# Two steps for the outputs of a chunk: a one-element read by ScalarE in place of a drain of TensorE

## Chip, cores and metric

The kernel runs on one core of a Trainium2 chip. The metric is the device time of one execution in microseconds. Before the change three runs took 586.36, 588.10 and 589.55 us, median 588.1.

## What is computed

A DeltaNet recurrence over 768 tokens for 4 batches of 8 heads of size 48, and then a multiplicative feed-forward block over the 3072 tokens that it yields:

```python
def _attn_ref(q, k, v, beta):               # (4, 8, 768, 48), beta (4, 8, 768)
    k_n = k / (np.linalg.norm(k, axis=-1, keepdims=True) + 1e-06)
    state = np.zeros((B, H, D, D), dtype=np.float32)
    for t in range(S):
        kt, vt, bt = (k_n[:, :, t], v[:, :, t], beta[:, :, t, None])
        y[:, :, t] = np.einsum('bhd,bhde->bhe', q[:, :, t], state)
        v_old = np.einsum('bhde,bhd->bhe', state, kt)
        state = state + bt[:, :, :, None] * np.einsum('bhd,bhe->bhde', kt, vt - v_old)

def _moe_ref(x, w1, w2, w3, w_out):         # x (3072, 384), w1 and w2 384 x 1024
    return ((x @ w1) * (x @ w2) @ w3) @ w_out
```

## The kernel before

**Tiling.** The 768 tokens are cut into 12 chunks of 64 (`c` or `m` in the code). Two chunks make a unit `u` of 512 tokens (4 batches times 128), with which the feed-forward block works. Within a chunk the recurrence is written in matrix form: scores K K^T and K Q^T, the inverse of a triangular matrix, the product of that inverse with (V minus K times the state), the new state, and the outputs.

**Order.** Every part of the work is a Python generator that yields after each step. The string `ORDER` names the parts in the order in which their steps are issued: a letter for the part and a number for the chunk, unit or block. `step` runs one step, and `in_text_order` (L177) chains the instructions of each engine in this order, so no scheduler moves them. Each engine works through its own queue in this order and waits for the others by semaphores; the DMAs are issued by SP, in its own order.

The parts that matter here:
- `s` scores (L378): for each of two halves r a group of 48-row TensorE products (L388, L394) into a bank pair, then VectorE takes U (L400) and PT (L418) out of it.
- `e` corner (L500) completes the inverse with small TensorE products (L522), `c` chain (L567) makes the state's products, the product of the inverse (R times T) and the new state, all at L575 with two or three bank pairs.
- `y` outputs (L639), the part that is changed.
- `V` inverse of 32x32 blocks, on VectorE (L462, L469).
- `b`, `a` products of x with w1 and w2 (L808), with copies by ScalarE (L823) and multiplications by VectorE (L827).
- `A`, `B` (L888 to L942) the same for a pair of 128-row blocks of w1 or w2 with eleven half products in place of more (a Strassen-like scheme): TensorE L897, ScalarE L902 to L918, VectorE L922 and L928. They need the sums of `m` (L876 by GpSimd, L879 by VectorE).
- `S` sums of slabs by GpSimd (L1000), `o` products with the folded weights w3 w_out (L1028), `x` results (VectorE L1059, ScalarE L1063 and L1065) and their stores (L1045, SP).
- `f` fold of w3 and w_out (L788, copies by ScalarE L795), `t` transposes (L779), `k`, `q`, `v`, `p`, `P` loads.

**Banks.** `two_banks` (L164) hands out one of two PSUM bank pairs in turn, `bank` (L167) one of four single banks in turn. A part that takes a pair waits, by the framework's dependences, until all readers of the pair's last contents are done. The scores, the corner, the chain and the outputs all take pairs; the first two inverses hold one of the two for a time.

**Tiled and dense products.** The recurrence's products have at most 64 rows and columns of weights; TensorE works four of them at a time in its quadrants (here "tiled"). The feed-forward block's products use 128 x 128 weights ("dense").

**The outputs.** y of chunk c is the sum of two things: Q times the state (48 rows, L672, operands `KQ,S`) and PT times X (64 rows, operands `PT,X`). The sums of a bank may come from products that lie in different row halves of TensorE. The kernel therefore makes two lists, `modes`: the first has the state products of the lower half and all PT products, the second the state products of the upper half. All products of the first list are issued, then a drain of TensorE (L670), and then the second list. In the next step of the part ScalarE copies the sums into xT in eight pieces (L693), and in a third (chunk 0 and every odd chunk) SP issues six DMAs that move rows within xT (L704), which GpSimd's and VectorE's sums (L876, L879) and the first products of the next pairs (L897) read. Chunk 0 has no state, so only its first list holds products; its drain has nothing behind it.

A product is two instructions for TensorE (a weight load and a matmul, each issued twice for float32), so the first list is 32 + 64 instructions and the second 32.

Of the kernel before, what the change touches and what calls it, by code (L numbers as in the profile page):

```python
# [8 lines left out]
FP32 = mybir.dt.float32  # L9
# [27 lines left out]


ORDER = """
k0 g0 beta beta g0 g0 P0 K0 C1 beta C1 g0 C0 C0 q0 k1 g0 K0 P4 K1 g0 g0 g0 K0 K0 C9 C9 C0 K1 C8  # L40
C1 P5 C8 K1 k2 C8 K1 g0 K1 K0 q1 C10 C11 t0 t0 Q0 Q0 P1 C10 Q0 Q0 Q0 k3 C11 g0 Q1 Q1 Q1 C9 t1
N0 C10 P6 Q1 Q1 N0 g1 C11 P9 C3 C2 C3 g1 C3 g1 s0 C2 C2 P2 s0 s0 s0 t3 C13 C12 C12 C18 N0 s0 g1
C19 C12 s0 s0 s1 s1 t1 C18 C5 t2 t2 q3 s1 C19 u0 C13 C13 C18 g1 P3 t3 C6 s1 s1 C19 s1 u1 P8 f0
C7 t4 C5 V0 V0 t5 g1 C4 C7 C4 v0 C5 g1 C4 C6 C6 C7 f1 P7 V0 f0 n0 C17 C17 v1 V0 V0 V0 V0 V0 V0
V0 V0 V0 V0 V0 V0 V0 V0 V0 V0 V0 C16 P10 C16 t4 V0 t5 V0 V0 V0 V0 f0 f1 f1 C17 t10 t10 V0 V0 V0
t11 K2 s1 C14 t11 K2 f5 f5 C15 V0 C15 C16 V0 C14 V0 g1 V0 K2 t9 V0 K2 f5 P11 C20 V0 C14 C20 V0
t8 C15 t9 K2 f2 q2 f2 V0 C21 n0 C23 C21 V0 C21 Q3 V0 f2 t8 Q3 Q3 V0 V0 V0 V0 V0 V0 V0 V0 V0 V0
V0 V0 V0 V0 V0 V0 V0 V0 V0 V0 V0 V0 t13 t6 V0 V0 V0 V0 t13 f4 P13 f4 t6 C26 C20 Q3 Q3 g1 t12
P12 f4 t7 V0 V0 V0 V0 g1 V0 Q2 t12 N1 t7 Q2 C27 K3 Q2 Q2 e0 C27 Q2 e0 C22 C22 C26 f6 s2 e0 s2
e0 C23 K3 e1 s2 f3 C24 K3 C23 K3 e0 s0 C25 s2 C25 e0 C22 p4 C26 V1 s2 c0 s2 u2 C24 e1 e1 C27 c0  # L50
P14 t15 e1 c0 y0 K3 c0 y0 s3 s3 s3 t14 s3 f3 C29 s3 u3 e1 s3 t14 V1 c1 C24 e1 f6 V1 n1 n1 c1 c1
c1 f6 V1 V1 V1 V1 V1 C28 f7 t15 f7 f7 C28 C28 C29 s1 y1 V1 V1 V1 V1 f3 y0 b0 C25 C29 b0 y1 b5
V1 b6 b6 P15 V1 V1 V1 V1 V1 V1 V1 V1 V1 V1 V1 V1 V1 V1 V1 V1 V1 V1 b5 P16 y1 b7 v2 b3 b1 C30 b7
b2 P17 C32 n2 b3 n2 V1 V1 V1 V1 V1 V1 V1 V1 V1 V1 V1 V1 c1 d4 V1 a05 V1 V1 b1 a02 V1 V1 V1 V1
V1 C31 a02 V1 k4 b2 V1 V1 V1 V1 V1 V1 V1 a05 a06 V1 b4 a04 a04 b4 V1 a07 C30 C30 C32 C32 a06
a00 V1 V1 V1 V1 V1 V1 a01 V1 V1 a07 a03 c1 d4 C34 a00 c2 C34 C35 C35 C34 a01 C31 C33 C33 b3 C33
C31 a03 a03 C35 a01 p4 e2 a03 b1 a01 T T b3 T b1 a00 b0 e2 e2 e2 d4 b0 N1 a00 b6 c2 e2 g2 b5 d4
b5 T v3 n3 n3 W2 e2 e3 N1 c2 b4 b6 c2 a05 y2 e3 b4 a05 a04 a04 y2 k5 a07 g2 g2 g2 g2 e3 W2 c2
a07 b7 b2 e3 e3 c2 c3 a06 g2 g2 g2 S0 p5 b7 g2 d5 d5 p5 k6 c3 V2 e3 S0 b2 c3 c3 a02 g2 a02 y3
o0 W2 N2 s4 W1 a06 W1 W1 y3 s4 y3 s4 s4 s4 o0 u4 d5 d5 s5 s4 s5 S0 S0 s5 s5 S0 m1 x0 s5 m1 o0  # L60
u5 S0 S0 S0 S0 S0 S0 S0 S0 S0 x0 x0 m1 m1 g3 g3 g3 g3 o0 o0 x0 V2 c3 V2 V2 o0 V2 B10 V2 x0 B10
V2 x0 S0 S0 o0 x0 V2 V2 V2 x0 V2 B10 V2 B10 x0 B10 B10 B10 B10 B10 x0 V2 V2 A10 v5 V2 A10 B10
B10 A10 A10 A10 A10 B10 A10 V2 B10 p6 A11 A11 A11 A11 A11 A10 A10 V2 A11 V2 V2 V2 V2 V2 A10 A11
A10 A10 A11 A11 A11 A10 d6 A12 A12 k7 v4 A12 A12 A12 d6 A12 A12 A11 V2 V2 V2 A12 A12 A12 V2 V2
A12 V2 A12 B10 B12 B12 A11 B10 p6 B12 V2 A12 B12 B12 B12 B12 V2 x0 V2 V2 B12 V2 B12 W1 A13 A13
B12 B12 A11 B12 B12 B12 B12 N2 V2 N2 A13 d6 A13 e4 s5 c3 n4 d6 A13 p7 B11 B11 B11 B11 B11 B11
B11 B11 g3 g3 g3 g3 B11 B11 B11 c4 n4 A13 S1 g3 B11 e4 e4 e4 c4 A13 A13 A13 e4 g3 A13 N3 e5 A13
e4 s6 c4 s6 s6 c4 A13 y4 a16 B11 d7 y4 s6 d7 p7 e5 e5 a16 N3 B11 B11 o1 A13 s6 u6 S1 N3 s6 n5
n5 e5 c4 d7 a17 d7 c4 a17 S1 x1 s7 s7 s7 V3 s7 s7 o1 c5 s7 e5 S1 o1 S1 S1 S1 S1 c5 e5 c5 S1 S1
S1 c5 u7 V3 S1 S1 o1 x1 V3 V3 V3 V3 S1 y5 p8 o1 x1 S1 V3 V3 V3 V3 x1 y5 o1 V3 c5 V3 V3 V3 v6 x1  # L70
y5 x1 x1 x1 S1 c5 A22 A22 m2 m2 o1 m2 d8 d8 x1 V3 n6 x1 m2 A22 A22 A22 A22 A22 A22 A22 B20 B20
V3 B20 B20 A22 B20 V3 V3 A22 A22 B20 B20 k8 V3 A20 g4 A22 A20 B20 B20 V3 V3 V3 A20 B20 x1 A20
A20 A20 A20 A20 V3 B20 A20 p8 A20 A21 V3 V3 V3 A20 A20 B20 B22 A20 A21 B20 A21 A21 B20 B20 B22
c6 v7 V3 V3 V3 V3 V3 B22 B22 V3 V3 k9 V3 B22 B22 A21 A21 A21 B22 B22 B22 A21 A21 B22 B22 B22
B22 A21 A21 d8 A21 B21 B22 B21 B21 g4 e6 g4 A23 A21 B22 B21 A23 B21 A23 g4 g4 g4 d8 p9 A23 g4
g4 A23 A23 e7 e6 B21 B21 B21 B21 B21 B21 n6 c6 e6 A23 e6 A23 A23 g4 e6 s8 e6 A23 g4 N4 A23 B21
B21 B21 c6 a26 n7 s8 s8 e7 c6 A23 B21 y6 y6 d9 d9 s8 A23 v8 a27 a27 a26 n8 S2 S2 o2 s8 V4 s8 c6
e7 n7 S2 p9 d9 e7 u8 o2 c6 d9 s9 s9 s9 n8 s9 s9 s9 x2 o2 x2 e7 e7 c7 S2 u9 V4 c7 S2 S2 S2 S2 x2
o2 c7 S2 S2 S2 S2 S2 S2 c7 o2 V4 V4 V4 V4 V4 y7 y7 x2 V4 y7 S2 S2 V4 o2 V4 V4 x2 x2 o2 A30 A30
V4 V4 V4 x2 m3 x2 x2 m3 V4 p10 m3 V4 c7 x2 V4 m3 k10 A30 A30 A30 A30 A30 A30 A30 V4 A31 A31 V4  # L80
A31 A30 A30 A30 c7 A31 k11 A31 A31 A32 A31 A31 A31 V4 V4 V4 A31 A31 c8 A31 V4 A30 A32 V4 A32
B30 A31 A32 V4 V4 V4 V4 V4 V4 V4 V4 V4 A32 A32 A32 A32 B30 B30 B30 B30 B30 B30 B30 B30 B30 B30
v9 A32 A32 V4 B30 B32 B30 A32 A32 B30 B32 B32 B30 B32 A32 A33 d10 B32 B32 g5 B32 A33 x2 n9 B32
B32 n9 d10 A33 c8 A33 A33 A33 e8 B32 B32 e8 B32 N4 e8 B32 B32 N4 a36 e8 e8 g5 g5 e8 g5 A33 c8
A33 g5 A33 p10 A33 c8 B31 d10 c8 y8 A33 B31 d10 c8 B31 B32 B31 B31 A33 e9 e9 B31 B31 B31 g5 a36
g5 g5 y8 e9 B31 S3 p11 e9 g5 B31 B31 B31 d11 d11 e9 B31 B31 S3 V5 c9 B31 e9 c9 A33 a37 c9 o3 c9
y9 a37 g5 s10 N5 s10 p11 s10 v10 y9 y9 d11 d11 o3 x3 s10 s11 S3 S3 s10 s10 s11 s11 s11 s11 m4
m4 m4 m4 u10 S3 S3 S3 S3 S3 S3 S3 S3 u11 o3 V5 x3 S3 S3 S3 S3 s11 n10 o3 x3 o3 x3 A40 V5 V5 o3
V5 A40 c9 x3 x3 V5 V5 o3 x3 x3 A40 V5 x3 V5 V5 A40 A40 A40 A40 A40 A40 x3 V5 V5 V5 A40 A43 A43
A43 A40 V5 A40 A43 A43 A43 A40 A43 A43 A43 B40 A43 V5 V5 V5 A43 B40 V5 V5 A43 B40 B40 B40 B40  # L90
A42 A43 V5 V5 V5 V5 A42 B40 B40 B40 B40 A42 A42 A42 A42 B40 B40 A42 a46 A42 V5 V5 B40 B40 B40
B42 A42 A42 c9 v11 a46 A42 V5 B42 A42 A42 V5 V5 B42 B42 V5 V5 B42 V5 V5 V5 V5 e10 A41 B42 n10
B42 B42 B42 A41 A41 B42 B42 B42 B42 B42 x3 A41 A41 A41 c10 A41 B41 A41 B41 A41 A41 A41 B41 c10
A41 n11 e10 B42 B41 B41 B41 B41 B41 B41 B41 e10 B41 S4 B41 B41 B41 e10 e10 e10 S4 a47 A41 e11
e11 B41 e11 a47 e11 c10 N5 N5 o4 c10 x4 e11 c10 c10 e11 o4 o4 S4 S4 S4 S4 n11 S4 S4 S4 y10 y10
x4 c11 o4 c11 c11 S4 S4 S4 S4 S4 o4 c11 x4 y11 S4 S4 x4 y11 o4 x4 x4 o4 y11 A50 A50 x4 x4 m5
# [10 lines left out]
def kernel(  # L107
# [14 lines left out]
    P = 128  # L122
# [5 lines left out]
    NP = H // 2  # L128
# [19 lines left out]
    def feat(z):  # L148
        return slice(C * z, C * z + D)
# [6 lines left out]
    def in_turn(pool, shape, tag, n, name, dt=FP32):  # L156

        i = turns.get(tag, -1)
        while True:
            i = turns[tag] = (i + 1) % n  # L160
            if (tag, i) not in held:
                return pool.tile(shape, dt, tag=f"{tag}{i}", name=name, bufs=1)
# [24 lines left out]

    ident = const.tile([P, P], FP32, name="ident")
    make_identity(nc, ident[:])
    strict = in_turn(ffn, [P, P], "o", 2, "strict")  # L190
    pool.memset(strict[:], 1.0)
    pool.affine_select(
# [72 lines left out]
    sums = {}  # L265
# [373 lines left out]
    def outputs(c):  # L639
# [24 lines left out]
                            x = half((z + h) % 2)  # L664
                            todo.append((h, z, r, X[x, r, h, :], PT[x, r, h, :]))
        part = [(h // NP, (h + z) % 2) for todo in modes for h, z, *_ in todo]
        issued, n = ([], []), 0
        for mode, todo in enumerate(modes):
            if mode:
                drain = pe.drain().ins  # L670
            for h, z, r, lhs, rhs in todo:
                i = pe.matmul(  # L672
                    region(h, z, r), lhsT=lhs, rhs=rhs,
                    start=part[n] not in part[:n], stop=part[n] not in part[n + 1 :],
                )
                issued[mode].append(i.ins)
                n += 1
        for i in issued[0]:
            in_order(i, drain)
        for i in issued[1]:  # L680
            in_order(drain, i)
        yield
        u, cc = divmod(c, 2)
        if cc == 0:
# [529 lines left out]
```

## Time and profile before

| what | value |
|---|---|
| runs, us | 586.36, 588.10, 589.55 |
| profiled execution, us | 585.52 |
| its span, us | 583.8 |
| mean granted TensorE clock | 0.977 |
| L672 `KQ,S`: matmuls | 704 in chunks 1 to 11, 14.8 us busy |
| L672 `PT,X`: matmuls | 768, 14.0 us busy |
| L693 copies to xT by ScalarE | 96, 366 ns each, 30.5 us busy |
| L704 DMAs within xT | 42; to landing 1.9, 2.6, 5.4 us (shortest, median, longest) |
| L1028 products, dense, 192 columns | 330 ns each, issued at a distance of 0.16 us |

The profiled execution took 585.52 us, of which 583.8 are the span from the first to the last instruction. Matmul lengths are modelled and overlap, so that distances between the starts of weight loads (`PEld`) tell more of TensorE's pace than the lengths of its matmuls. In the lists of groups and in timelines, `<-` names what ended the idle time before an instruction.

### The profile page before, as it was taken

What the parts mean: (1) busy time and instruction counts of PE and PEld (TensorE: products, weight loads), DVE (VectorE), ACT (ScalarE), POOL (GpSimd) and SP (SyncE); (2) the same over time, 40 slices, a digit from 0 to 9 for tenths busy, and PEclk for the clock granted to TensorE, in tenths of its full rate; (3) what the DMA queues carried; (4) which work ended last, traced back from release to release, by engine and by line L of the source; (5) the groups of instructions that cost most, each with busy time, mean ns of one, the idle gap of its engine ahead of it and who ended that gap; (6) DMA issues with size and microseconds to landing.
All of it is one profiled execution on the core that took longest, in us unless ns stands there. A gap on an engine that the chain in (4) does not pass through costs nothing.

```text
span 583.8 us, 20142 instructions
## 1 busy us (share of the span) xinstructions
PE 536.8 (92%) x8660; PEld 419.4 (72%) x8660; DVE 357.9 (61%) x828; ACT 194.3 (33%) x449; POOL 222.7 (38%) x284
## 2 busy tenths in 40 slices
PE   4559796899999999999999999999999999989997
PEld 3546464678888975678877688676688767977787
DVE  2645956379546689854898664985485974123522
ACT  2776674344432012331133222123421323323310
POOL 6476407032778703536105371024325043610041
PEclk9669999899999999999999999999999999999999
DMA  8999955778764436444472533455434103010001
GB/s 231 223 274 245 245 121 82 120 143 140 129 94 67 96 74 103 92 58 90 94 124 66 84 47 71 86 122 77 55 66 98 26 37 70 10 50 15 0 1 54
DMA packets 204408, 56.59 MB, mean 97 GB/s; under 512 B 193344, under 2 KB 199488, under 8 KB 202528
## 3 DMA queue, kind: packets, MB, share of 16 engines
q1 hardware_dynamic: 200128, 54.52, 48.0%
q10 hardware_dynamic: 4192, 0.79, 0.9%
q8 instruction: 68, 1.11, 0.8%
q14 instruction: 20, 0.16, 0.1%
HBM read 43.09 MB, written 11.01 MB: 93 GB/s over the span
## 4 chain that ended last, share of the span: by engine, by line
PE 76%; DMA 13%; DVE 3%; ACT 3%; SPq 3%; issue 2%; ACTq 0%; DVEq 0%
PE ps_f L897 29%; PE ps_f L1028 15%; PE ps_f L808 11%; PE ps_w L575 6%; PE ps_w L672 4%; PE ps_f L788 4%; DMA raw<-in_moe_w_dram 3%; PE ps_w L522 3%; DMA X<-in_q_dram 2%; DMA Ub<-Ud 2%; DMA Ud<-U 1%; PE ps_w L388 1%; PE ps_w L394 1%; DMA raw<-in_moe_w_out_dram 1%; DMA vtok<-in_v_dram 1%
## 5 line engine op out<-in xcount | busy, mean ns | idle before, releaser
L1000 POOL TENSOR_TENSOR ab<-ab 128x256 f32<-128x256 f32 x96 | 68.2, 740 | 59.6 <-DVE ab L942 35.1
L942 POOL TENSOR_TENSOR ab<-ab,y 128x512 f32<-128x512 f32 x24 | 30.5, 1272 | 130.3 <-DVE y L922 81.3
L897 PE MATMUL ps_f<-xT,w1s 128*128 128x256 f32 (+1 forms) x200 | 70.3, 471 | 0.3 <-DVE ab L928 0.2
L1028 PE MATMUL ps_f<-w,ab 128*128 128x192 f32 x376 | 66.0, 330 | 4.2 <-DVE osb L1059 4.2
L1028 PEld LDWEIGHTS ps_f<-w,ab 128*128 128x128 f32 x376 | 60.9, 190 | 6.5 <-issue 5.7
L897 PE MATMUL ps_f<-xT,w2s 128*128 128x256 f32 (+1 forms) x160 | 56.3, 468 | 0.1
L897 PEld LDWEIGHTS ps_f<-xT,w1s 128*128 128x128 f32 x200 | 36.8, 190 | 24.7 <-issue 19.4
L693 ACT COPY xT<-ps_w 48x256 f32<-48x256 f32 x96 | 30.5, 366 | 70.5 <-PE ps_w L672 70.0
L1028 PE MATMUL ps_f<-room,ab 128*128 128x192 f32 x272 | 48.2, 331 | 2.4 <-DVE room L1059 2.4
L788 PE MATMUL ps_f<-w2s,w3T 128*128 128x384 f32 x128 | 46.4, 514 | 3.7 <-ACT KQ L368 2.5
L469 DVE TENSOR_TENSOR Vb<-Vb,tb 128x31 f32<-128x31 f32 (+15 forms) x124 | 45.1, 364 | 4.3
L462 DVE TENSOR_TENSOR tb<-Vb,Ub 128x31 f32<-128x31 f32 (+15 forms) x124 | 43.4, 350 | 5.7 <-DMA Ub<-Ud 2.9
L1028 PEld LDWEIGHTS ps_f<-room,ab 128*128 128x128 f32 x272 | 44.0, 190 | 3.8 <-issue 2.4
L808 PE MATMUL ps_f<-xT,w2s 128*128 128x256 f32 (+1 forms) x144 | 45.5, 461 | 0.0
L897 PEld LDWEIGHTS ps_f<-xT,w2s 128*128 128x128 f32 x160 | 29.8, 190 | 19.2 <-issue 15.3
L788 PEld LDWEIGHTS ps_f<-w2s,w3T 128*128 128x128 f32 x128 | 24.5, 198 | 20.4 <-ACT KQ L368 3.1
L808 PEld LDWEIGHTS ps_f<-xT,w2s 128*128 128x128 f32 x144 | 26.1, 189 | 10.6 <-issue 7.7
L388 PE MATMUL ps_w<-KQ 48*64 48x128 f32 x384 | 26.8, 284 | 7.5 <-ACT PT L412 6.3
L740 POOL TENSOR_TENSOR w<-w,raw 128x512 uint32<-128x512 uint32 x16 | 20.4, 1287 | 31.4 <-DVE w L738 27.7
L388 PEld LDWEIGHTS ps_w<-KQ 48*64 48x64 f32 x384 | 22.2, 140 | 11.9 <-ACT PT L412 6.7
L897 PE MATMUL ps_f<-xT,room 128*128 128x256 f32 x100 | 29.8, 385 | 0.1
L561 POOL TENSOR_TENSOR vtok<-vtok,n 128x384 f32<-128x384 f32 x24 | 19.9, 838 | 23.5 <-DMA vtok<-in_v_dram 23.5
(155 smaller groups left out, 983.0 us busy)
## 6 DMA issues: line engine op xcount, KB each, us to landing
raw<-in_moe_w_dram SPq DMA_DIRECT2D x8, 1024.0 KB, 8.2
vtok<-in_v_dram SPq DMA_DIRECT2D x24, 192.0 KB, 4.4
raw<-in_moe_w_dram SPq DMA_DIRECT2D x12, 384.0 KB, 7.7
out_dram<-osb SPq DMA_DIRECT2D x46, 96.0 KB, 1.7
ktok<-in_k_dram SPq DMA_DIRECT2D x44, 96.0 KB, 4.1
raw<-in_moe_w_out_dram SPq DMA_DIRECT2D x4, 768.0 KB, 4.9
Ud<-U SPq DMA_DIRECT2D x48, 64.0 KB, 3.1
Ub<-Ud SPq DMA_DIRECT2D x6, 512.0 KB, 3.8
```

The lines of the kernel that those rows point to most:

```text
L388: pe.matmul(ps[half(z), 0, n : n + 128], lhsT=x[:, 0, :], rhs=x.rearrange("p j t -> p (j t)"), start=True, stop=True,)
L462: dve.tensor_tensor(out=tv, in0=V[:, 0 : s + 1, s : s + 1].to_broadcast([P, s + 1, n]), in1=U[:, s, s + 1 : BS].unsqueeze(1).to_broadcast( ...
L469: dve.tensor_tensor(out=o, in0=o, in1=tv, op=ALU.subtract)
L575: pe.matmul(out(ps, r, h, z), lhsT=lhs(r, h, z), rhs=rhs(r, h, z), start=True, stop=True,)
L672: i = pe.matmul(region(h, z, r), lhsT=lhs, rhs=rhs, start=part[n] not in part[:n], stop=part[n] not in part[n + 1 :],)
L693: act.copy(out=xT[f, p:NP:2, b : b + NR, cc, :].rearrange("p a r t -> p r a t"), in_=pyv[f, z, b : b + NR],)
L788: pe.matmul(ps[:, 0:DM], lhsT=w3Ts[jc, kc // 4][:, kc % 4 * P : kc % 4 * P + P], rhs=wo[:, kc], start=(kc == 0), stop=(kc == KF - 1),)
L808: pe.matmul(ps[:].rearrange("p b c t -> p b (c t)"), lhsT=w[:, m, js], rhs=x[:, m, :, c0:c1].rearrange("p b c t -> p b (c t)"), start=(m = ...
L897: pe.matmul(ps, lhsT=lhs, rhs=rhs, start=start, stop=stop, skip_group_check=not start)
L942: (dve if u == last else pool).tensor_tensor(out=t, in0=t, in1=y[i], op=ALU.mult)
L1000: pool.tensor_tensor(out=o_, in0=x_, in1=y_, op=op)
L1028: pe.matmul(ps[b][:, b, :], lhsT=abs_[u, HF * f + i][:, t0 : t0 + P], rhs=ws_[w][:, i], start=first and i == 0 and (b == 0 or n == "F"), s ...
```

## The change

The drain goes. For chunks with a state (1 to 11) `outputs` has two more steps: after the first list it yields; then ScalarE copies one element of the region that the last product of the first list wrote into a small tile, `seen`, and yields; then the second list is issued, its first product with a dependence on that read. The other steps follow as before. Since the second list now adds onto finished groups, the `stop` flags are set at the end of the first list, and the second list skips the check of groups.

```diff
+    seen = const.tile([P, 1], FP32, name="seen")
...
-        issued, n = ([], []), 0
+        n = 0
         for mode, todo in enumerate(modes):
-            if mode:
-                drain = pe.drain().ins
-            for h, z, r, lhs, rhs in todo:
+            if mode and todo:
+                yield
+                h, z, r = modes[0][-1][:3]
+                read = act.copy(
+                    out=seen[feat(h // NP)][0:1], in_=region(h, z, r)[0:1, 0:1]
+                ).ins
+                yield
+            for x, (h, z, r, lhs, rhs) in enumerate(todo):
                 i = pe.matmul(
                     region(h, z, r), lhsT=lhs, rhs=rhs,
-                    start=part[n] not in part[:n], stop=part[n] not in part[n + 1 :],
-                )
-                issued[mode].append(i.ins)
+                    start=part[n] not in part[:n],
+                    stop=part[n] not in part[n + 1 : len(modes[0]) if mode == 0 else None],
+                    skip_group_check=mode == 1,
+                ).ins
+                if mode and x == 0:
+                    tc.add_manual_dep(
+                        i, read.name,
+                        mybir.DependencyInfo(mybir.DependencyClass.Sync, mybir.DependencyReason.DATA),
+                        reason="sums of both modes",
+                    )
                 n += 1
-        for i in issued[0]:
-            in_order(i, drain)
-        for i in issued[1]:
-            in_order(drain, i)
         yield
```

`ORDER` keeps all other tokens in their order and gets 22 more `y` tokens. The first list and the read stand where the whole step stood; the second list stands some tokens later, and the copies where they stood or, where that would be ahead of the second list, behind it. Two places, before and after (`y3` has its DMAs as a last step, `y9` too):

```
before  y3 o0 W2 N2 s4 W1 a06 W1 W1 y3 s4 y3 s4 s4 s4
after   y3 y3 o0 y3 W2 N2 s4 W1 a06 W1 W1 y3 s4 y3 s4 s4 s4

before  y9 a37 g5 s10 N5 s10 p11 s10 v10 y9 y9 d11 d11 o3 x3 s10 s11
after   y9 y9 a37 g5 s10 N5 s10 p11 s10 v10 d11 d11 o3 y9 y9 y9 x3 s10 s11
```

What lies on TensorE between the first and the second list, and what follows the second list:

| chunk | between | behind |
|---|---|---|
| 1 | 3 dense products (b, 256 columns) | dense (b) |
| 2 | 3 dense (a, 256) | 3 dense (a), corner products, then the state's (L575) |
| 3 | 8 dense (o, 192) | scores, first and second half |
| 4 | 3 dense (a, 512) | scores, second half, then corner products (L522) |
| 5 | 8 dense (o, 192) | dense (o), L575, then the first pair product (L897) |
| 6 | scores (first half), 3 dense (a, 512) | 8 dense (o), then the state's (L575) |
| 7 | 8 dense (o, 192) | dense (o), then the first pair product (L897) |
| 8 | 2 dense (pair, 256) | dense (pair) |
| 9 | scores (first half), 8 dense (o, 192) | scores, second half, and of the next chunk |
| 10 | L575 (state), 8 dense (o, 192) | L575 (R times T) |
| 11 | 8 dense (o, 192) | dense (o), then the first pair product (L897) |

The orders of SP, VectorE and GpSimd are unchanged; ScalarE has the eleven reads more, in chunk 1 between two fold copies (L795), and in chunk 10 a copy of a result (L1065) stands ahead of the eight copies in place of behind them, in chunk 8 the order of the eight copies and the pair's copies is as before.

## Prediction, made before the run

> **What bounds the kernel now.** I read the page first: its busy shares, the 40 slices and the chain of work that ended last.
>
> ```profile
> span 583.8 us, 20142 instructions
> PE 536.8 (92%) x8660; PEld 419.4 (72%) x8660; DVE 357.9 (61%) x828; ACT 194.3 (33%) x449; POOL 222.7 (38%) x284
> PE   4559796899999999999999999999999999989997
> ...
> PE 76%; DMA 13%; DVE 3%; ACT 3%; SPq 3%; issue 2%; ACTq 0%; DVEq 0%
> ```
>
> TensorE is busy nine tenths or more in almost every slice (14.6 us each) from the ninth on, and three quarters of the chain are its own work. So a microsecond in which TensorE stands still after about 100 us is a microsecond of the result, unless it falls where TensorE waits anyway. All eleven drains (chunks 1 to 11) lie behind 124 us.
>
> Next, one drain from near: the timeline of weight loads (PEld) around chunk 9, and ScalarE's in the same stretch. Columns are start, length, engine, line, operation, operands, shapes, count.
>
> ```profile
> 425.23 0.52 PEld L672 LDWEIGHTS ps_w<-KQ,S 48*48 48x48 f32 x32 [0.23 <-PE ps_f L1028]
> 425.66 0.98 PEld L672 LDWEIGHTS ps_w<-PT,X 64*48 64x48 f32 x64
> 426.90 0.52 PEld L672 LDWEIGHTS ps_w<-KQ,S 48*48 48x48 f32 x32 [0.26 <-issue]
> ...
> 428.43 2.57 PEld L1028 LDWEIGHTS ps_f<-room,ab 128*128 128x128 f32 x16
> 431.23 0.14 PEld L388 LDWEIGHTS ps_w<-KQ 48*64 48x64 f32 x2 [0.23 <-issue]
> ```
>
> ```profile
> 427.64 2.59 ACT L693 COPY xT<-ps_w 48x256 f32<-48x256 f32 x8 [8.70 <-PE ps_w L672]
> ```
>
> The first sums are the first two rows, the second sums the third. A load takes 0.12, so the last load of the first sums starts at 425.66 + 0.98 - 0.12 = 426.52 and the next one at 426.90: the drain makes this distance 0.38, where the first two rows join at 0.03. The dense L1028 loads (0.19 each) end with one that starts at 430.81; the tiled L388 follows 0.42 later, though dense loads of this form follow each other at 0.16. A change between dense and tiled products is thus paid too. Eight copies of 2.59 in all empty the bank pair: from the first load of the second sums (426.90) to the end of the copies (430.23) it is 3.33.
>
> **The change on TensorE alone.** Eleven distances of 0.38 go: -4.18. In chunks 1, 2, 5, 6, 7, 8 and 11 the second sums become a tiled group of their own between dense products. Such a group costs, beside its own loads, 0.52 (last dense load of 256 columns to the first tiled one) + 0.20 (tiled to dense) + 0.11 (first to second dense load), less the two dense distances of 0.22 that would stand there: 0.40, and the same with 192 and 512 columns (0.42 and 0.95 in place of 0.52, with 0.16 and 0.43). Seven of them: +2.8. In chunks 3, 4, 9 and 10 the second sums join tiled work that follows (four joints of 0.03: +0.1). Sum -1.3. The places below are worked out with absolute starts, so this sum is inside them and isn't added again. ScalarE's eleven reads of one element have no row; the nearest are its copies, 0.37 for 256 columns and 0.48 for 384, so 0 to 0.37 each; I take 0.2. ScalarE is mostly idle at those places (8.70 in the row above), and at least two dense products on TensorE cover each read.
>
> **What moves: the copies.** They start 0.74 after the first load of the second sums (426.90 to 427.64), now later by a whole dense group, and two things wait for them.
>
> First, the bank pair. There are two, taken in turn, so the second taker after a chunk's outputs needs its pair. Chunk 0 shows the rule at work, with TensorE idle:
>
> ```profile
> 105.16 2.59 ACT L693 COPY xT<-ps_w 48x256 f32<-48x256 f32 x8 [4.26 <-PE ps_w L672]
> ```
> ```profile
> 106.70 0.66 PE L779 MATMUL ps_f<-ident,w 128*128 128x128 f32 x4
> 107.81 0.33 PE L388 MATMUL ps_w<-KQ 48*64 48x128 f32 x2 [0.45 <-ACT xT L693]
> ```
>
> The copies end at 107.75, all eight of them, and the scores start at 107.81. So the second taker starts no earlier than 3.33 + 0.06 = 3.39 after the first load of the second sums. Before, 2.6 to 2.8 us of dense products stood in this time; now they stand ahead of the second sums. In the times of the profile of before:
> - Chunk 9: the tiled scores and the dense group behind the drain move up by 0.78; the last dense load starts at 430.03, the second sums at 430.45, the second scores at 433.84 in place of 431.23: +2.6.
> - Chunk 10: last dense load 508.75, second sums 509.16, R times T (L575) 512.55 in place of 509.95: +2.6.
> - Chunk 4: second sums 256.85 (0.95 behind a 512-column load), corner products (L522) 260.24 in place of 258.52: +1.7.
> - Chunk 3: second sums 186.60, second scores 189.99 in place of 188.68: +1.3.
> - Chunk 2: second sums 169.57, state products (L575) 172.96 in place of 172.22: +0.7.
>
> Chunk 6 also has a second taker, reached 0.1 too late to wait. Sum 8.9.
>
> Second, the transfers. After the odd chunks six DMAs (L704) move rows of xT, POOL (L876) takes the first pieces, and the next pairs' first product (L897) needs the same pieces. Chunk 7:
>
> ```profile
> 361.94 2.59 ACT L693 COPY xT<-ps_w 48x256 f32<-48x256 f32 x8 [8.78 <-PE ps_w L672]
> 363.06 2.57 PEld L1028 LDWEIGHTS ps_f<-room,ab 128*128 128x128 f32 x16 [1.33 <-issue]
> 363.90 3.73 SPq L704 DMA_DIRECT2D xT<-xT  x6
> 367.91 0.94 POOL L876 TENSOR_TENSOR room<-xT 128x256 f32<-128x256 f32 x1 [14.77 <-DMA xT<-xT]
> 369.77 0.35 PEld L897 LDWEIGHTS ps_f<-xT,w1s 128*128 128x128 f32 x2
> ```
>
> From the start of the copies to the pieces it is 5.97 here, 5.96 in chunk 11 (516.23 to 522.19), 6.97 in chunk 5 (281.61 to 288.58): 6.7 to 7.7 from the second sums' first load.
> - Chunk 7: the dense group stays at 363.06, for it waits for VectorE; second sums 365.86, pieces 372.56, L897 in place of 369.77: +2.8.
> - Chunk 11: second sums 518.11, pieces 524.81 in place of 522.80: +2.0.
> - Chunk 5: second sums 283.50, pieces 290.2 to 291.2 in place of 288.99: +1.2 to +2.2, I take 1.7.
>
> Here the drain does go into an idle second (TensorE waits 1 us for VectorE at 285.12), and the transfer takes it back. Sum 6.5. SP's queue keeps its order; the stores of results (L1045) behind the six DMAs come later by as much as TensorE.
>
> Third, two small ones. In chunk 1 the read stands ahead of a fold copy (L795, 0.43) that frees the bank of the next dense product: first sums end about 126.1, read 0.2, copy 0.43, so that product starts about 0.7 late. In chunk 8 a copy of L902 (0.37) behind the read holds the second product: 0.3. Sum 1.0; bounds 0.3 and 1.5.
>
> All together 8.9 + 6.5 + 1.0 = 16.4. The profiled run took 585.5 with a span of 583.8, so 601.9 by its own time. The runs' median, 588.1, lies 2.6 above it: 604.5 by the median.
>
> **The clock.** Standing still also costs speed. Stretches of the profile of before, with busy time (and count) of PE first and the granted clock behind POOL's:
>
> ```profile
> 95.87:99.28 3.41, 2.27 (x128) 1.94 (x128) 3.24 (x5) 0.04 (x1) 3.35 (x5) 1.00 0.70 94
> 99.28:106.11 6.83, 5.59 (x156) 5.05 (x160) 0.96 (x1) 2.53 (x7) 2.34 (x3) 0.50 0.64 98
> 362.10:365.50 3.40, 2.41 (x15) 2.44 (x16) 3.14 (x10) 2.39 (x8) 0.00 (x0) 1.00 0.04 10
> ```
>
> After 3.41 us with 2.27 of tiled products only, the clock was halved for 6.83. After 3.40 with 2.41 of dense products it wasn't. The new idle times of 1.3 to 2.8 lie beside tiled work: 3.4 us from the second sums of chunk 9 or 10 hold 0.5 to 0.7 of tiled products and nothing else, well under the first row. So I expect falls at the seven waits of over a microsecond, where the clock's windows happen to fit; a fall of 3.41 over work that TensorE bounds loses half of it, 1.7, one of 6.83 loses 3.4. Bounds: none (0) and all seven at 1.7 (12). I take about 3.5 at 1.7: +6, since the nearest row did fall. Forecast 604.5 + 6, say 610.
>
> The Trainium skill, page "TensorE: Matmul & The Clock Gate", section "HAM oscillation — how this bites in real kernels", puts the rule as no idle gaps of TensorE over about 3.4 us; by it none of these waits would slow the clock. The first row above doesn't agree: there the longest pause in the 3.41 us was 1.1 us.
>
> **Rivals.**
> 1. The waits come, the clock holds, since every new idle time is under 3 us: 604.5. For it: 205.10 to 208.50 (2.09 busy, dense) kept the full clock. Against it: the row at 95.87. The skill's rule just named is this rival. Chance 0.25.
> 2. Only the copies or only the transfers bite, because what is late is absorbed further on (the pair phase of L897 has small waits on ScalarE): 588.1 + 8 to 10 = 597. Against it: TensorE's large waits after 200 us are on VectorE steps that themselves follow TensorE's products. Chance 0.08.
> 3. The other side: the bank pair comes free piece by piece, so that the second taker waits for one copy of 0.37 and not for eight, and the transfers' delay falls into idle time. Then TensorE's own -1.3 is left: 586.8, no difference; if the dense joints too cost nothing, -4.2: 583.9. It decides where the second taker starts less than 1 us after the copies begin. Against it: chunk 0, where the taker started 0.06 after the eighth. Chance 0.07.
>
> My forecast has 0.6. Range 600 to 620: the low end is 1 and a light case of the waits, the high end six or more falls of the clock. About 0.5% (2.9 us) is what a measurement can tell from no change here. Faster 0.03 and same 0.04 are rival 3, slower 0.93 the rest.
>
> **What would show it.** In the timeline of after: no 0.38 distance behind the first sums; L388, L522 and L575 behind the outputs of chunks 2, 3, 4, 9 and 10 with idle time put down to ScalarE's xT copies (L693 of before), 0.7 to 2.6 each; the first L897 of chunks 5, 7 and 11 waiting for DMA xT<-xT; stretches after 180 us at a clock of 0.50; ScalarE's reads at 0.2 or so. I am wrong if the second taker starts before the eighth copy ends, if L897 isn't held, or if TensorE's idle time after 120 us grows by less than 10.

## The result and the profile after

The changed kernel took 612.1 us (median of six runs, 605.3 to 616.4), the kernel before beside it 587.2 (585.3 to 589.8): a ratio of 1.038, 95% interval 1.031 to 1.045. Ratios, here and below, leave out executions over 1.5% above the fastest of the same kernel: two of these six, and in the split of the chunks 6, 9 and 10 below the profiled one, which took 790.0 us at a granted clock of 0.653, so that its stages can't be compared. The prediction was 610. The changed kernel's profiled execution has a span of 611.2 us against 583.8, so 27.4 more.

The page of the changed kernel, whose lines stand three to eleven further down than before (L672 is L680, the copies L693 are L704, the DMAs within xT L704 are L715, L388 is L391, L522 is L525, L575 is L578, L897 is L908):

```profile
span 611.2 us, 20140 instructions
PE 551.7 (90%) x8660; PEld 428.4 (70%) x8660; DVE 359.4 (59%) x828; ACT 195.4 (32%) x460; POOL 222.9 (36%) x284
PE   3669898899998999989899989899989999879997
PEclk9669797999998999989999999899989999999999
```

The clock's row of the page before:

```profile
PEclk9669999899999999999999999999999999999999
```

TensorE's share falls from 92% to 90%, and eights stand in its row where there were nines; the clock's row, all nines behind the eighth slice before, has eights too. Both together are the result, and two stretches tell them apart. First before, then after, cut at the first weight load of chunk 1's first sums (the columns are start and end, length, busy time and count of PE, PEld, DVE, ACT and POOL, granted clock, share and rate of the DMA):

```profile
124.60:583.80 459.20, 445.23 (x6973) 354.35 (x6972) 289.38 (x653) 122.59 (x316) 166.28 (x217) 1.00 0.40 72
```
```profile
126.00:611.20 485.20, 456.14 (x6973) 361.93 (x6972) 288.98 (x649) 124.12 (x327) 165.23 (x216) 0.98 0.37 68
```

The same 6973 matmuls take 10.9 us more of busy time, at a clock of 0.98 in place of 1.00; TensorE's idle time grows from 459.20 - 445.23 = 14.0 to 485.20 - 456.14 = 29.1, by 15.1. The sum, 26.0, is the whole difference but for 1.4 that was there before chunk 1. So three fifths of the loss are waits and two fifths are longer work, nearly all of it by the clock: the six falls listed below, of 3.41 at half speed, can make up 10.2 of the 10.9.

What TensorE newly waited for, five rows from the list of its waits (line, releaser, total, times, longest):

```profile
PE ps_f L908 <- DMA xT<-xT: 6.7, 3, 2.4
PE ps_w L391 <- ACT xT L704: 5.4, 3, 2.7
PE ps_w L578 <- ACT xT L704: 3.2, 2, 2.7
PE ps_w L391 <- DVE S L638: 2.0, 1, 2.0
PE ps_w L525 <- ACT xT L704: 1.8, 1, 1.8
```

One of the three at L391 (0.90) is chunk 0's, which stood in the profile before too (0.45). The rest are the chunks 2, 3, 4, 9 and 10 for the copies (0.51, 1.77, 1.76, 2.71, 2.69), and 5, 7 and 11 for the transfer (1.85, 2.42, 2.42). The wait for S is new in kind: chunk 6. How a place looks from near, at chunk 9: TensorE's weight loads and ScalarE's row.

```profile
443.65 2.57 PEld L1039 LDWEIGHTS ps_f<-room,ab 128*128 128x128 f32 x16
446.45 0.52 PEld L680 LDWEIGHTS ps_w<-KQ,S 48*48 48x48 f32 x32 [0.23 <-issue]
449.82 0.14 PEld L391 LDWEIGHTS ps_w<-KQ 48*64 48x64 f32 x2 [2.86 <-ACT xT L704]
```
```profile
442.92 0.15 ACT L675 COPY seen<-ps_w 1x1 f32<-1x1 f32 x1 [7.99 <-PE ps_w L680]
447.18 2.59 ACT L704 COPY xT<-ps_w 48x256 f32<-48x256 f32 x8 [4.11 <-PE ps_w L680]
```

The read was over at 443.07, three microseconds before anybody needed it. The second sums load at 446.45, behind the dense group; the eight copies end at 449.77, and the next taker of the bank pair starts at 449.82, 3.37 after the second sums. Nothing is slow here; everything is late.

The clock was at 0.50 for 3.41 us at 194.4, 266.1, 385.5, 450.4, 532.3 and 549.4, each time 0.2 to 1.4 us behind the end of one of these waits (chunks 3, 4, 7, 9, 10, 11). Before it stayed at 1.00 from 106 us to the last instructions.

### The profile page after: what moved, and what is told of

It is laid out like the page before. It is cut to its first block, busy times and chain, and to the rows that moved or that the text cites. A ratio compares the mean times of both kernels' runs of the same rounds, so it can differ in the third digit from the quotient of the medians.

```text
span 611.2 us, 20140 instructions
## 1 busy us (share of the span) xinstructions
PE 551.7 (90%) x8660; PEld 428.4 (70%) x8660; DVE 359.4 (59%) x828; ACT 195.4 (32%) x460; POOL 222.9 (36%) x284
## 4 chain that ended last, share of the span: by engine, by line
PE 69%; ACT 4%; DMA 3%; DVE 2%; SPq 2%; issue 1%; POOL 0%; ACTq 0%; DVEq 0%; POOLq 0%
PE ps_f L908 29%; PE ps_f L1039 15%; PE ps_f L819 11%; PE ps_w L578 5%; PE ps_w L680 4%; ACT xT L704 3%; PE ps_w L525 2%; PE ps_w L391 1%; PE ps_f L799 1%; PE ps_w L397 1%; DMA xT<-xT 1%; DMA Ud<-U 1%; SPq L254 1%; SPq L715 1%; PE ps_w L1039 1%
## 5 line engine op out<-in xcount | busy, mean ns | idle before, releaser
L908 PE MATMUL ps_f<-xT,w1s 128*128 128x256 f32 (+1 forms) x200 | 71.4, 476 | 7.0 <-DMA xT<-xT 6.7
L1039 PE MATMUL ps_f<-w,ab 128*128 128x192 f32 x376 | 67.5, 334 | 3.1 <-DVE osb L1070 3.0
L908 PEld LDWEIGHTS ps_f<-xT,w1s 128*128 128x128 f32 x200 | 37.3, 193 | 32.5 <-issue 26.4
L908 PE MATMUL ps_f<-xT,w2s 128*128 128x256 f32 (+1 forms) x160 | 56.3, 468 | 0.1
L799 PE MATMUL ps_f<-w2s,w3T 128*128 128x384 f32 x128 | 50.9, 553 | 4.3 <-ACT KQ L371 3.8
L1039 PE MATMUL ps_f<-room,ab 128*128 128x192 f32 x272 | 50.9, 343 | 1.3 <-DVE room L1070 1.3
L1039 PEld LDWEIGHTS ps_f<-room,ab 128*128 128x128 f32 x272 | 46.6, 199 | 2.5 <-issue 1.1
L908 PEld LDWEIGHTS ps_f<-xT,w2s 128*128 128x128 f32 x160 | 29.8, 190 | 19.2 <-issue 15.3
L799 PEld LDWEIGHTS ps_f<-w2s,w3T 128*128 128x128 f32 x128 | 26.3, 214 | 23.9 <-issue 6.2
L704 ACT COPY xT<-ps_w 48x256 f32<-48x256 f32 x96 | 30.5, 365 | 34.6 <-PE ps_w L680 34.1
L391 PE MATMUL ps_w<-KQ 48*64 48x128 f32 x384 | 28.4, 294 | 13.3 <-ACT PT L415 5.7
L391 PEld LDWEIGHTS ps_w<-KQ 48*64 48x64 f32 x384 | 23.5, 146 | 16.9 <-ACT PT L415 6.3
L348 DVE STREAM_TRANSPOSE KQ<-perm 128x512 f32<-128x512 f32 x32 | 21.3, 690 | 19.6 <-PE ps_w L680 11.6
L908 PE MATMUL ps_f<-xT,room 128*128 128x256 f32 x100 | 30.8, 395 | 0.1
```

Of the source, the lines that this page charges most:

```text
L391: pe.matmul(ps[half(z), 0, n : n + 128], lhsT=x[:, 0, :], rhs=x.rearrange("p j t -> p (j t)"), start=True, stop=True,)
L704: act.copy(out=xT[f, p:NP:2, b : b + NR, cc, :].rearrange("p a r t -> p r a t"), in_=pyv[f, z, b : b + NR],)
L799: pe.matmul(ps[:, 0:DM], lhsT=w3Ts[jc, kc // 4][:, kc % 4 * P : kc % 4 * P + P], rhs=wo[:, kc], start=(kc == 0), stop=(kc == KF - 1),)
L908: pe.matmul(ps, lhsT=lhs, rhs=rhs, start=start, stop=stop, skip_group_check=not start)
L1039: pe.matmul(ps[b][:, b, :], lhsT=abs_[u, HF * f + i][:, t0 : t0 + P], rhs=ws_[w][:, i], start=first and i == 0 and (b == 0 or n == "F"), s ...
```

## Experiments

Numbers of waits and clock falls are those of each run's profiled execution. A "stage" of chunk n runs from the first weight load of its first sums to that of the next chunk's (for chunk 11 to TensorE's last load), and is compared with the same stage of the kernel before. Where a kernel changes nothing in a stage, the stages from 2 on mostly differ by -0.4 to +0.4. Stage 7 is less steady, from 1.3 shorter to 2.2 longer, since TensorE waits for VectorE in it by more or less (1.21 and 1.33 in the kernel before) and the clock fell in it once without a change; stage 3 was once 1.4 longer. Ahead of chunk 2 kernels differ by more (the start of chunk 1 by up to 4.6, its stage by up to 5.7), and nothing is read there.

### One kind of chunk at a time

Four kernels in which only some chunks are computed in two steps. All others drain and have their steps where the kernel before has them. Against the changed kernel:

```diff
+SPLIT = (2, 3, 4, 9, 10)
...
         for mode, todo in enumerate(modes):
-            if mode and todo:
+            if mode and c not in SPLIT:
+                drain = pe.drain().ins
+            elif mode and todo:
                 yield
```

The copies' chunks:

> Only the chunks 2, 3, 4, 9 and 10 (those behind whose second sums the next taker of the bank pair stood waiting for the ScalarE copies) are computed in two steps; all others drain as before. Theory: every chunk pays its own wait, whatever the others do. In the profile of the changed kernel these five waits were 0.5 + 1.8 + 1.8 + 2.7 + 2.7 = 9.4 us, and four falls of the granted clock stood directly behind the chunks 3, 4, 9 and 10, at 1.0 to 1.7 us each: +13 to +16, that is 600 to 604 beside a kernel before of 587, with the same five waits for the copies in the trace and none for the transfer. Rival, the split as such (reads and one more tiled group) costs the same at every chunk: 24.9/11 = 2.3 us each, +11, 598.5, and waits that are much smaller than 9.4 together. Rival, the falls are set off only by all pauses together: +9.4, 596.6, no fall behind 120 us.

The transfers' chunks:

> Only the chunks 5, 7 and 11 (those whose transfer within xT came too late for the first pair product) are computed in two steps. Theory: their waits were 1.85 + 2.4 + 2.4 = 6.7 us, and two falls of the clock stood behind 7 and 11, at 1.0 to 1.7 each: +8.5 to +10, 596 to 597.5; no wait of TensorE for the xT copies over 0.3 us. Rival of an even price for each chunk: 3 x 2.3 = +7, 594. Rival, clock falls only from all pauses together: +6.7, 594, without a fall behind 120 us.

Chunk 6:

> Only chunk 6 is computed in two steps. Theory: the transposes of chunk 9 into the KQ buffer that chunk 6 still reads wait for its second sums, and VectorE's queue stands behind them; TensorE then waits for PT (0.6), S (2.0) and KQ (0.2): +3 to +3.4, 590 to 590.6, with a wait of about 2 us for S behind chunk 6 and no other new wait. Rival, an even price: +2.3, 589.5, and no wait for VectorE there. Rival, chunk 6 only came late in the changed kernel because the work ahead of it was 10 us late already: +0, 587.

Chunks 1 and 8:

> Only the chunks 1 and 8 are computed in two steps: behind them the changed kernel had no wait but 0.8 us at chunk 1. Theory: a drain of 0.38 less and one change from dense to tiled products of 0.40 more for each, and 0.8: +0.5 to +1, 588, within what can be measured of the kernel before. Rival, an even price for each chunk of 2.3: +4.6, 592.

| split | time, us | ratio to before, 95% interval | new waits, us |
|---|---|---|---|
| 2, 3, 4, 9, 10 | 599.0 | 1.0175 (1.0135 to 1.0215) | 0.52, 1.78, 1.77, 2.71, 2.70 |
| 5, 7, 11 | 597.6 | 1.0204 (1.0174 to 1.0233) | 1.84, 2.43, 2.42 |
| 6 | 589.1 | 1.0054 (1.0027 to 1.0081) | 0.64, 1.79 |
| 1, 8 | 588.1 | 1.0023 (0.9996 to 1.0050) | 0.77 |

The four excesses add up to 4.6% against the whole change's 3.8% (3.1 to 4.5), which their own intervals allow, and each wait comes back to within 0.2 us. In the lists of waits, the first kernel:

```profile
PE ps_w L391 <- ACT xT L713: 5.3, 3, 2.7
PE ps_w L578 <- ACT xT L713: 3.2, 2, 2.7
PE ps_w L525 <- ACT xT L713: 1.8, 1, 1.8
```

and the second, which has no such waits but chunk 0's:

```profile
PE ps_f L917 <- DMA xT<-xT: 6.7, 3, 2.4
```

So each chunk pays by itself, and an even price for each chunk (2.3) is out: it would be 4.6 for 1 and 8, which cost 1.4 by their ratio and at most 2.9 by its interval. That it is the transfer which holds the first pair product rests on this division and on the releaser that the traces name; no run made the transfer itself shorter. The clock falls divided in the same way. The first kernel had four behind 120 us, at the chunks 3, 4, 9 and 10 (those at 3 and 4 lasted 6.83 in this execution, which took 603.2, more than the median); the second had two, at 7 and 11; the third had none.

### Late because of whom?

The copies' and transfers' tokens moved to where the changed kernel has them, but no split:

```diff
-y9 a37 g5 s10 N5 s10 p11 s10 v10 y9 y9 d11 d11 o3
+y9 a37 g5 s10 N5 s10 p11 s10 v10 d11 d11 o3 y9 y9
```

> No split: the drains stay and both lists of sums stand where the kernel before has them; only the eight copies of every chunk (and the transfers within xT) are moved to the places that the changed kernel gives them in the queues of ScalarE and SyncE. Theory: the copies were late because the second sums stood late in TensorE's order, not because of their place in ScalarE's queue: few instructions are passed there, so 586 to 589 beside 586.5, each of the waits for the xT copies or for the transfer under 0.6 us. Rival: the place in the queues is what made them late: waits of 9.4 (copies) and 6.7 (transfers) as in the changed kernel, 603 to 610.

587.0 against 587.0 (ratio 1.0014, 0.9984 to 1.0045), no wait for copies but chunk 0's, none of L917 for the transfer, no clock fall between 106 us and the last instructions. (One of 0.9 for chunk 1's transfer, at L828, also comes and goes in other kernels that leave chunk 1 as it was: 0.75 with chunk 6 alone split, 1.25 in the filled kernel with 594.3 us below.) What came late was the second sums in TensorE's own order; the places in the other queues are free.

The read in the drain's place, with the second sums directly behind it:

```diff
-y9 y9 a37 g5 s10 N5 s10 p11 s10 v10 d11 d11 o3 y9 y9 y9
+y9 y9 y9 a37 g5 s10 N5 s10 p11 s10 v10 y9 y9 d11 d11 o3
```

> All eleven chunks are split, but the second sums stand directly behind the read, with no dense product between: the read takes the drain's place and nothing else moves. Theory: nothing is late in this kernel, so it costs only what the read takes more or less than a drain. The drain left 0.38 us between the last first sum and the first second one; the read takes 0.15 by itself, with two hand-overs and whatever ScalarE is doing when it comes: 0.4 to 0.9 between them, so 0 to +6, 586.5 to 592.5, and no new waits for copies over 0.6. Rival: the read as such is what cost the time (2.3 a chunk): 611.

588.5 against 587.0 (1.0027, 0.9999 to 1.0055). ScalarE's reads, in the group of the tile `seen` (shortest, median and longest in ns, first and last start):

```profile
L674 ACT COPY seen<-ps_w x11: 150/150/152, 128.2 to 519.3; 1x1 f32<-1x1 f32 x11
```

From the last load of the first sums to the first of the second it is now 0.52 to 0.60, where the drain has 0.38: the read takes 0.15 and the two hand-overs the rest. That is 0.14 to 0.22 for each of eleven chunks, 2 us in all. A read in the open is a little dearer than a drain; the change's loss isn't the read.

### The copies as the price of the bank pair

The kernel that splits 2, 3, 4, 9 and 10, with four of the eight copies on VectorE:

```diff
-                    act.copy(
+                    copy = dve.tensor_copy if p and c in SPLIT else act.copy
+                    copy(
                         out=xT[f, p:NP:2, b : b + NR, cc, :].rearrange("p a r t -> p r a t"),
```

> As the kernel that splits the chunks 2, 3, 4, 9 and 10 alone (599, waits for the copies of 0.5, 1.8, 1.8, 2.7 and 2.7), but four of the eight copies of these chunks are made by VectorE beside ScalarE's four. Theory: the next taker of the bank pair waits for the last copy, and eight in a row on ScalarE take some 2.7 us; four and four take about half, so each wait falls by 1.0 to 1.4: 0, 0.5, 0.5, 1.5 and 1.5, some 4 in all, and fewer falls of the clock: 591 to 595; VectorE's own queue stands behind the second sums then, which can give up to 1 back. Rival: the taker waits for the second sums and not for the copies: waits stay at 9.4, 599.

It went the other way: 612.5 (1.0446, 1.0417 to 1.0475). Chunk 9, VectorE's and ScalarE's rows:

```profile
445.54 0.42 DVE L714 COPY xT<-ps_w 48x256 f32<-48x256 f32 x1 [0.62 <-ACT xT L714]
446.39 0.43 DVE L714 COPY xT<-ps_w 48x256 f32<-48x256 f32 x1 [0.43 <-ACT xT L714]
```
```profile
445.14 0.37 ACT L714 COPY xT<-ps_w 48x256 f32<-48x256 f32 x1 [4.17 <-PE ps_w L683]
445.99 0.37 ACT L714 COPY xT<-ps_w 48x256 f32<-48x256 f32 x1 [0.48 <-DVE xT L714]
```

The two engines take turns, each waiting for the other's copy, so the chain of eight is 3.39 long (445.14 to 448.53) in place of 2.59. The expectation of a shorter chain fails, but the disputed rule is tested all the same: a chain 0.8 longer made the waits of the chunks 2, 3 and 9 longer by 0.89 each (1.41, 2.67, 3.60), so the taker waits for the last copy and not for the sums. At chunk 4 TensorE now waits 4.17 for VectorE's T, which stands behind the copies in VectorE's queue, and at chunk 10 it waits 4.65 in place of 2.70: the copies held other work up.

### Chunk 6

VectorE in the changed kernel (before, the first of these rows followed the sums at 335.67, with 3.31 idle):

```profile
349.06 1.30 DVE L348 STREAM_TRANSPOSE KQ<-perm 128x512 f32<-128x512 f32 x2 [6.84 <-PE ps_w L680]
...
352.18 0.68 DVE L403 TENSOR_TENSOR U<-ps_w,wt 128x512 f32<-128x512 f32 x1
352.78 0.68 DVE L421 TENSOR_TENSOR PT<-ps_w,smask 128x512 f32<-128x512 f32 x1
357.43 0.71 DVE L348 STREAM_TRANSPOSE KQ<-perm 128x512 f32<-128x512 f32 x1 [3.97 <-DMA Ud<-U]
358.06 0.92 DVE L638 TENSOR_TENSOR S<-S,ps_w 128x768 f32<-128x768 f32 x1
```

There are three KQ buffers, and chunk 9's transposes write the one from which chunk 6's second sums still read. They wait for those sums, and U and PT queue behind them; SP loads the next rows for the transposes only when the first two have read theirs, so the third transpose comes late as well, with the addition into S behind it. TensorE then waited 0.64 for PT and 1.96 for S.

A first try at moving the third transpose behind that addition (token `d9` behind `u8`):

> As the kernel in which chunk 6 alone was split, but the third of chunk 9's four transposes into KQ is put behind chunk 8's state update in VectorE's order. Theory: the wait of TensorE for S (1.8 us in that run) came from the state update standing behind a transpose that waited for the q transfer, itself late by the second sums: that wait goes, under 0.3 us, the wait for PT of 0.6 stays, and the time falls from 589.1 by 1.5 to 2, to 587 to 587.6. Rival: S was late because TensorE gave its part of it late: the wait stays at 1.8 and the time at 589.

591.8 (1.0076, 1.0043 to 1.0109), waits 0.64 and 1.57. It tells nothing of the theory: the addition is issued by `c6`, two tokens further on, so the transpose still stood ahead of it. It serves as a second run of the split of chunk 6 alone. The move done properly:

```diff
-p9 d9 e7 u8 o2 c6 d9
+p9 e7 u8 o2 c6 d9 d9
```

> As the kernel that splits chunk 6 alone (589.1, and again 591.8 in the run where the moved transpose was still ahead of the state update), but the third of chunk 9's transposes into KQ now stands behind the addition into S in VectorE's order. Theory: TensorE's wait for S (1.8 and 1.6 us there) came from that transpose, held by the q transfer, standing ahead of the addition: the wait falls under 0.3, the 0.64 for PT stays, the stage from chunk 6 to chunk 7 is longer than before by 1.2 to 1.8 instead of 3.0 to 3.3, 587.3 to 588. Rival: the addition itself is late for its products: the wait stays at 1.6 to 1.8.

589.9 (1.0042, 1.0010 to 1.0073). VectorE:

```profile
347.34 0.94 DVE L638 TENSOR_TENSOR S<-S,ps_w 128x768 f32<-128x768 f32 x1
351.45 1.30 DVE L348 STREAM_TRANSPOSE KQ<-perm 128x512 f32<-128x512 f32 x2 [3.17 <-DMA Ud<-U]
```

The addition is 4 us earlier against the work around it, and TensorE's wait for S is gone, as the theory has it. But the next scores read what the transposes write, and wait 1.27 for KQ in its place; the stage is 2.6 longer than before, where the split without this move had 3.0 and 3.3. So the chain through the KQ buffer and VectorE's queue is shown; the expectation that the addition's place alone would give the time back was wrong.

### The clock, and a place where the split pays

Three dense products in front of the first pair product behind chunks 7 and 11, in the kernel that splits 5, 7 and 11; their result is overwritten.

```diff
         Q, q_held = held_bank()
+        if p == 0 and u in (3, 5):
+            for _ in range(3):
+                product(Q[:], A11, w[:, 0, 0:NT], True, True)
         product(Q[:, hi], A11, B11, True, True)
```

> As the kernel that splits the chunks 5, 7 and 11 alone (597.6; waits for the transfer of 2.4 at 7 and at 11, a fall of the clock to 0.50 for 3.4 us behind each), but three dense products of 128x512, whose result is overwritten, stand ahead of the first pair product behind chunk 7 and behind chunk 11: 2.2 us of work in each pause of 2.4. Theory: the transfer lands when it did, so the wait as such stays in the time, but the clock finds no pause and does not fall: the stage behind 7 (3.5 longer than before) and the one behind 11 (4.2 longer) each shrink by 1.2 to 1.75, 594 to 595.2. Rival: the falls have another cause than the pause: both stay, and the time is 597.6 or, where the filling is late itself, more.

598.4 (1.0190, 1.0136 to 1.0243), not shorter. `eleven` runs twice for each unit, once with w1 and once with w2, so the three products also stood in front of the second group, where there is no pause, for 2.58 each time. Behind 11 the clock didn't fall, and the stage was 5.06 longer than before: 4.18 + 2.58 would be 6.76, so 1.70 were saved. Stage 7 can't be read (the clock fell at 368.7, ahead of the second sums, behind a wait of 2.06 for VectorE).

The second try has the filling once, and in the same kernel the chunks 6, 9 and 10 with their second sums directly behind the tiled group that follows the outputs anyway:

```diff
-        if p == 0 and u in (3, 5):
+        if p == 0 and u in (3, 5) and w is w1s:
...
-y6 y6 d9 d9 s8 A23
+y6 y6 s8 y6 y6 d9 d9 A23
...
-y9 a37 g5 s10 N5 s10 p11 s10 v10 y9 y9 d11
+y9 y9 a37 g5 s10 y9 N5 s10 p11 s10 v10 y9 y9 d11
...
-y10 y10 x4 c11 o4
+y10 y10 x4 c11 y10 y10 o4
```

> Two questions in one kernel, at different chunks. (a) Chunks 5, 7 and 11 are split as in the changed kernel, and three dense products (2.6 us, result overwritten) fill the pause behind 7 and behind 11, this time in front of the first of the two groups of pair products only; the run before had them in front of both, so that 2.6 us stood in the open each time, and its stage behind 11 was 5.06 longer than before where the split without filling had 4.18: 4.18 + 2.58 - 1.70. Theory: a pause of 2.4 sets off a fall, and the fall costs 1.7 beside the pause: the stage behind 11 is 2.3 to 2.8 longer than before, the one behind 7 1.7 to 2.3, no fall within 5 us behind either. Rival, the filling only changes the order: 4.2 and 3.5 with falls, or 5 without them. (b) Chunks 6, 9 and 10 are split with the second sums behind the group of tiled products that follows anyway, the other chunks drain. Theory: the drain's 0.38 goes from each: the stages behind 6, 9 and 10 are 0.2 to 0.4 shorter than before (beside the 0 to 0.1 that stages without a change differ), and no wait for copies over 0.3. Rival: the copies, 1 us later, hold the pairs: 0.6 longer behind 9 and 10. All in all 592.5 to 594.5 beside 587.

594.3 (1.0133, 1.0089 to 1.0177), where the same chunks without filling had 597.6. TensorE behind chunk 11:

```profile
524.49 2.74 PE L917 MATMUL ps_f<-w1s 128*128 128x512 f32 x6
527.06 0.67 PE L917 MATMUL ps_f<-xT,w1s 128*128 128x256 f32 x2
```

The pair product follows the filling without a wait, no fall follows 7 or 11, and their stages are 1.89 and 2.48 longer than before, in place of 3.50 and 4.18. At 11 that is 1.70 for a fall of 3.41, the same as in the first try. At 7 it isn't clean: a wait for VectorE ahead of the second sums was 0.62 here and 1.53 there. Chunk 5, whose pause of 1.84 wasn't filled, adds a test that wasn't planned: this time the clock fell behind it, and the stage was 2.75 longer; with the same pause and no fall it was 1.08.

```profile
283.00:289.30 6.30, 4.46 (x85) 4.08 (x84) 5.09 (x12) 2.17 (x8) 0.88 (x2) 1.00 0.16 34
289.30:292.70 3.40, 3.40 (x13) 3.40 (x12) 3.18 (x6) 0.22 (x1) 0.63 (x1) 0.50 0.55 146
```

And the same two stretches of the split of 5, 7 and 11 alone:

```profile
286.70:293.00 6.30, 4.46 (x85) 4.08 (x84) 5.11 (x12) 2.17 (x8) 0.85 (x2) 1.00 0.15 34
293.00:296.40 3.40, 3.37 (x20) 2.92 (x19) 3.21 (x7) 0.74 (x3) 0.95 (x1) 1.00 0.53 148
```

TensorE's work and pause ahead are the same to 0.00 us; behind them the clock differs. A fall of 3.41 costs 2.75 - 1.08 = 1.67.

The split behind tiled work alone, without the chunks 5, 7 and 11, had been run on its own:

> The kernel before, but in the chunks 6, 9 and 10 the drain is gone and the second sums stand behind the group of tiled products that follows anyway (scores of chunk 8, scores of chunk 10, products of chunk 11), with the read beside that group; chunk 9's transposes into KQ are moved behind the second sums of chunk 6. Every other chunk drains. Theory: no switch from dense to tiled products is added, the read is hidden, and each of the three saves the drain's 0.38; the copies come 1.0 us later, which their pairs' next takers have (0.9 us of room at 9 and 10), or wait 0.1 to 0.2 for: 0.6 to 1.1 less in all, 586 beside 587, inside what the times can tell, but to be seen in the stages, each 0.2 to 0.4 shorter, with no wait for copies over 0.3. Rival: the copies are late again and the takers wait 1 us each at 9 and 10: those stages 0.6 longer, 588.

588.1 against 587.5 (1.0004, 0.9970 to 1.0037): no difference. The stages, read in the run above, are 0.24 (6) and 0.26 (10) shorter than before, where kernels that drain there have 0.0; stage 9 is 0.11 longer, as in those (0.00 to 0.14). There is no wait for copies at any of them. Half a microsecond of 587 is all that the idea holds here, below what a median tells.

## Why the prediction was right, point by point

| chunk | next taker or pair product later by, predicted | measured | wait, us | stage longer by | fall behind it |
|---|---|---|---|---|---|
| 2 | 0.7 | 0.7 | 0.51 | 0.3 | no |
| 3 | 1.3 | 1.5 | 1.77 | 3.3 | yes |
| 4 | 1.7 | 1.3 | 1.76 | 2.7 | yes |
| 5 | 1.7 | 1.1 | 1.85 | 1.1 | no |
| 6 | 0 | - | 2.79 in three | 3.4 | no |
| 7 | 2.8 | 1.4 | 2.42 | 2.6 | yes |
| 9 | 2.6 | 2.6 | 2.71 | 3.4 | yes |
| 10 | 2.6 | 2.6 | 2.69 | 4.3 | yes |
| 11 | 2.0 | 1.9 | 2.42 | 3.8 | yes |

The third column is the start of the awaited product (or its weight load) after, less that before, less the shift of the chunk's first sums.

- **TensorE alone**: the 0.38 is gone and seven tiled groups have come in; chunk 8, with nothing else, is 0.1 longer. The read took 0.15 where 0.2 was taken, and its hand-overs are hidden. Of the two small terms, chunk 1's 0.7 came (a wait of 0.78), chunk 8's 0.3 did not.
- **The bank pair**: right. 3.37 after the second sums at chunk 9, where 3.39 was said; the five places gave 8.7 where 8.9 was said, and the run with the longer copy chain showed that it is the last copy that counts.
- **The transfers**: 1.1 + 1.4 + 1.9 = 4.4 in place of 6.5, the lack almost all at 5 and 7. Chunk 7's +2.8 rested on the dense group staying at 363.06 because it waited for VectorE. In the changed kernel TensorE came 3.4 later by chunk 6 and VectorE was nearly ready: the dense group started 2.19 behind the chunk's first load in place of 3.52, with 0.67 left of a wait of 1.21. With 5, 7 and 11 split alone the product came 2.3 later.
- **Chunk 6**: missed. "Reached 0.1 too late to wait" held for the bank pair, but the second sums have another reader's place to give up, the KQ buffer; +3.4 here, 3.0 and 3.3 alone. The prediction asked who waits for the copies, and not who waits for what the second sums read.
- **Sum of the waits**: 16.4 predicted, 15.1 more idle time measured. That they are so near is luck: chunk 6's 2.8, not forecast, are in the second, so the rest was some 4 too high. Of this 2.1 are the transfers and 0.56 a wait for PT behind chunk 9 that went when TensorE came later; what is left of it isn't traced to places. Rival 2's "absorbed further on" was true of a quarter at most, not of a half.
- **The clock**: forecast +6 from 3.5 falls of 1.7, with bounds of 0 and 12; there were six, and 10.9 more busy time. The price of one fall was right (1.67 and 1.70 measured), their number was the mis-sized term: seven candidates, of which I took half, and six fell. The reason given, pauses beside tiled work, isn't needed: behind chunk 11 the 3.41 us ahead of the fall (545.95 to 549.36) hold 0.85 us of dense work and no tiled. So rival 1 (604.5) is out. The Trainium skill's rule of no idle gaps over about 3.4 us (page "TensorE: Matmul & The Clock Gate", section "HAM oscillation — how this bites in real kernels") doesn't protect this kernel: behind 126 us no pause was over 2.71 us. The prediction's 1.1 us for the longest pause in the row at 95.87 is all of that row's idle time; its longest pause is 0.89, which speaks against the rule even more.
- **Rival 3** is out by the same rows: no second taker started ahead of the eighth copy.

Waits 1.3 below and the clock 4.9 above what was said, with 1.4 of start-up in this execution, make 27.4 of span; by the medians the change cost 24.9 where 22 was forecast.

## What to carry to other kernels

A wait that costs 0.38 in place can be cheap beside what moving its work sets off: ask of the moved instructions who waits for what they write and also who waits to overwrite what they read. Before counting a pause, look for a wait of the same engine further on that it will eat, and look at how much the engine works in the few microseconds around it: on an engine whose clock depends on being busy, a pause of 2.4 us cost 4. Split work only onto a neighbour that is of its own kind and already there.

## What the runs showed of the hardware

- Behind the split chunks every pause of TensorE of 2.4 us or more was followed or overlapped by a clock of 0.50 for 3.41 or 6.83 us: four in the changed kernel, two and two in the kernels with a part of it, four in the run with two copying engines. Of ten pauses of 1.76 to 1.96 it was five. The falls' starts in an execution lie at whole multiples of 3.41 us from each other (385.5, 450.4, 532.3, 549.4: 19, 24 and 5 of them), which fits fixed windows.
- Which pause is followed by a fall fits TensorE's busy time in one such window. All traces but the one at 0.653 were cut, from 126 us on, into stretches of 3.413 us counted from one of their falls. That gives 1730 stretches at full clock. A fall followed 21 of them, and in each of these TensorE was busy for at most 1.77 us; of the other 1709 only two had as little (1.56 and 1.77). Chunk 5 is the same pause at two places of this grid: 1.56 us busy with a fall behind it in the kernel with 594.3 us (285.90 to 289.31), 2.15 without one in the split of 5, 7 and 11 alone (290.86 to 294.27). So in that range it depends on how a pause lies to the windows' edges, which the kernel doesn't set. Busy time isn't all: the changed kernel's chunk 5 had 1.56 without a fall, and ahead of 126 us falls followed up to 2.27 of tiled work. No run was made to test this.
- Three dense products whose result is thrown away, put in a pause, kept the clock at 1.00 and saved 1.7 us behind chunk 11, twice.
- ScalarE and VectorE, copying different pieces of one bank pair into one tile, took turns. Whether the chip or the dependences between the instructions make them do so wasn't tried.
- Start-up varies: in kernels that change nothing ahead of it, chunk 1's first sums began between 3.0 us earlier and 4.6 us later than in the kernel before. Differences of a few microseconds are better read stage by stage than from two spans.
